# Retention and gated MLP on one core: scores and outputs on 64x64 quarters of TensorE, batch elements in its row halves

## The chip, the core and the metric

The kernel runs on one core of a Trainium2 chip. The core has five engines that run side by side and meet only at semaphores: TensorE (PE, matrix products), VectorE (DVE), ScalarE (ACT), GpSimd (POOL) and SyncE (SP, which here only issues DMAs). Each works through its own instructions in program order. The metric is the device time of one execution in microseconds (us). Before the change it is 214.01 us, the median of 3 runs (213.32 to 214.35).

## The reference

`q`, `k`, `v` have shape (4, 8, 768, 64): batch, heads, sequence, head dimension. Each head keeps a 64x64 state that decays by a factor of its own, and the result goes through an MLP:

```python
gamma = 1.0 - 2.0 ** (-5.0 - np.arange(H))
for t in range(S):
    state = gamma * state + k[:, :, t] (x) v[:, :, t]      # outer product
    y[:, :, t] = scale * q[:, :, t] @ state
...
x = y.transpose(0, 2, 1, 3).reshape(3072, 512)
h = x @ w_in                      # 512 -> 2048
g = h * np.cos(h)
return g @ w_out                  # 2048 -> 512
```

## The kernel before, in words

**Tiling.** The sequence is cut into 6 chunks of 128 positions and the batch into 2 pairs of elements, which makes 12 steps p (0 to 11) of one chunk and one batch pair. `ORDER` maps p to a chunk: p = 0 and 1 are the first chunks of the two pairs, so they have no state before them; all later steps have. Two steps make a group g (0 to 5) of 512 tokens, for which the MLP runs. Everything on PE is bf16, with float32 sums in PSUM. PSUM has 8 banks: one holds the state (`st_ps`), and seven are passed round first in, first out by `Banks`.

**One step p.** `load` brings q, k and v in float32. `conv_q`, `conv_k` and `conv_v` make bf16 copies and fold in the decay. q and k are transposed, by PE for p < 6 (`t_mm`, `t_copy`) and by a DMA issued on SP from p = 6 on (`dma_t`, line 297). `a_mm` (line 331) makes the scores A of a head: 64 rows of contraction, 128 keys by 128 queries. Head 2a stands in rows 0 to 63 and head 2a+1 in rows 64 to 127 of the transposed tiles, so two heads use the two row halves of the array at the same time, with an output bank for each; there are 16 such matmuls in a step. `a_mask` (line 337, DVE) multiplies by the causal mask. `y_mm` (lines 362 and 367) sums two products for each head: state times q, with a state padded by zeros to 128 rows (`stb`), and v times masked scores over 128 keys. Its outputs are 64 partitions high, so two heads stand in the two column halves; a step has 32 of these matmuls, 16 for each of the two products. `y_copy` (ACT) writes `xt`. `s_mm` (line 387) adds the chunk to the state, 16 matmuls of 64 columns, and `s_copy` (line 273 or 271) makes the bf16 state for the next step, in two halves.

**MLP.** `f_mm` (line 401) is one slice of 128 of the 2048 hidden features for 512 tokens, four matmuls of 512 columns; ACT takes the cosine (line 409), DVE multiplies (line 413). `h_mm` (line 422) does two slices for the 256 tokens of a single step, so it needs only that step. `o_mm` (line 446) is a quarter of the contraction of an output tile of 128 tokens; after four of them `o_out` copies the tile (ACT, `ob`) and issues its DMA on SP (line 455).

**The order.** The first part (p = 0 to 5, group 0, parts of p = 6 and 7) is ordered by a planner, `Plan`: each piece of work has a set of engines, a cost, what it comes after, a rank and the banks that it takes; the planner plays this through at build time and emits the pieces by planned start. Where PE would idle early, it puts in matmuls on zeros (`idle_mm`, line 472). In this part the q, k, v and weight loads are issued by POOL, and those of p = 0's k and p = 1's q and k (`"K"`, `"Q1"`, `"K1"`) convert to bf16 on the way. Then, in program order:

```python
plan.emit()
for p in (PL + 2, PL + 3):          # p = 8 and 9
    load(nc.sync, p, "q k v")       # six DMAs on SP
...
for g in range(2, NG + 1):
    for s in range(16):             # f_mm(g, s), then o_mm(g - 1, ...)
        if s % 4 == 3: o_out(g - 1, s // 4, "A")
        if p < NP and r == 3:       # s == 3 and s == 11
            block(p); conv(p + 2); load(nc.sync, p + 4, "q k v")
```

(cut; `conv` has the two `dma_t`, and `conv` and `load` are left out where p + 2 or p + 4 goes past 11.) `block(p)` issues the scores of p + 1, then Y of p with its copies, the state of p, and the masks of p + 1. It runs for p = 6 to 11. So SP's own queue holds, in order: the output DMAs of group 0, the six loads of p = 8 and 9, and then, for each block, an output DMA, two transposes, three loads (for p = 6 and 7) and another output DMA.

Of the kernel before, what the change touches and what calls it, by code (L numbers as in the profile page):

```python
# [146 lines left out]
HALF0, SPARE, RF, RM, COLD = 0, 1, 40.0, 40.0, 8.5  # L147
# [3 lines left out]
def kernel(  # L151
# [39 lines left out]
    st_ps = psum.tile([128, 2, HP, D], FP32, name="st_ps")  # L191
# [13 lines left out]
    qs = [sb([128, 2, H, D], BF16, f"qs{i}") for i in range(NB)]  # L205
    ks = [sb([128, 2, H, D], BF16, f"ks{i}") for i in range(NB)]
    vs = [sb([128, 2, H, D], BF16, f"vs{i}") for i in range(NB)]
    qkt = [sb([128, 2, 2, HP, 128], BF16, f"qkt{i}") for i in range(NB)]
    am = [[[sb([128, HP, 128], BF16, f"am{i}_{b}_{j}") for j in range(2)]
           for b in range(2)] for i in range(2)]  # L210
    stb = [sb([128, 2, HP, 128], BF16, f"stb{i}") for i in range(2)]
# [3 lines left out]
    kx = sb([128, 2, H, D], BF16, "kx")  # L215
# [10 lines left out]
    dec = gtf[:, 2048:4096].bitcast(FP32).rearrange("p (j a t) -> p j a t", j=2, a=HP)  # L226
# [13 lines left out]
    def load(eng, p, names):  # L240

        bp, c = divmod(ORDER[p], NC)
        for n in names.split():
            t, src = SRC[n[0].lower()]
            if len(n) == 1:
                t = (qs[p % NB] if n == "Q" else kb(p)) if n in "QK" else t[p % PRE]
                eng.dma_start(  # L247
                    out=t.rearrange("p b h d -> p (b h) d"),
                    in_=src[ds(2 * bp, 2), :, ds(c * C, C), :].rearrange(
                        "b h t d -> t (b h) d"))  # L250
            else:
                b = int(n[1])
                eng.dma_start(
                    out=t[p % PRE][:, b],
                    in_=src[2 * bp + b, :, ds(c * C, C)].rearrange("h t d -> t h d"))
# [22 lines left out]
    def conv_q(p, b, e):  # L278
        if p < 2:
            copy(e, qs[p % NB][:, b], qf[p % PRE][:, b])  # L280
            return
        ENG[e].tensor_tensor(out=qs[p % NB][:, b], in0=qf[p % PRE][:, b],  # L282
                             in1=bc(gq, ORDER[p] % NC), op=ALU.mult)
# [8 lines left out]
    def conv_k(p, b, e):  # L292
        copy(e, ks[p % NB][:, b], kf[p % PRE][:, b])

    def dma_t(p, w):
        n = p % NB
        nc.sync.dma_start_transpose(
            out=qkt[n][:, w].rearrange("p b a t -> p (b a) t"),
            in_=(qs, ks)[w][n].rearrange("p b h d -> p (b h d)"))
# [3 lines left out]
    def t_mm(p, b, w):  # L303
        if w == 0:
            held["t", p, b] = banks.take()
        tr = held["t", p, b].bitcast(BF16).rearrange("p (w a t) -> p w a t", w=2, a=HP)
        for a in range(HP):
            nc.tensor.transpose(  # L308
                tr[:, w, a, :], (kb(p) if w else qs[p % NB])[:, b, 2 * a : 2 * a + 2, :], ident)

    def t_copy(p, b, w, e):
        bank = held["t", p, b]
        tr = bank.bitcast(BF16).rearrange("p (w a t) -> p w a t", w=2, a=HP)
        copy(e, qkt[p % NB][:, w, b], tr[:, w])
# [3 lines left out]
    def qt(n, b, a):  # L318
        return qkt[n][:, 0, b, a, :]

    def kt(n, b, a):
        return qkt[n][:, 1, b, a, :]

    def a_mm(p, b):
        n = p % NB
        bk = held["a", p, b] = [banks.take(), banks.take()]
        ap = [t.rearrange("p (a t) -> p a t", a=HP) for t in bk]
        for a in range(HP):
            for j in range(2):
                po = 64 * j  # L330
                nc.tensor.matmul(ap[j][:, a, :], lhsT=kt(n, b, a)[po : po + 64, :],  # L331
                                 rhs=qt(n, b, a)[po : po + 64, :],
                                 tile_position=(po, 0))

    def a_mask(p, b, j):
        bank = held["a", p, b][j]
        nc.vector.tensor_tensor(  # L337
            out=am[p % 2][b][j], in0=bank.rearrange("p (a t) -> p a t", a=HP),
            in1=(dec[:, j] if p < 2 else mask.unsqueeze(1).to_broadcast([128, HP, 128])),
# [3 lines left out]
    def a_save(p, b, j):  # L343
        bank = held["a", p, b][j]
# [3 lines left out]
    def a_late(p, b, j):  # L348
        nc.gpsimd.tensor_tensor(out=am[p % 2][b][j],
                                in0=amf[b].rearrange("p (a t) -> p a t", a=HP),  # L350
                                in1=dec[:, j], op=ALU.mult)

    def y_mm(p, b):
        c = ORDER[p] % NC
        n = p % NB
        bank = held["y", p, b] = banks.take()
        v_ = vr[p] if p < 2 else vs[n]
        yp = bank.rearrange("p (a t) -> p a t", a=HP)
        for a in range(HP):
            if c > 0:  # L360
                for j in range(2):
                    nc.tensor.matmul(  # L362
                        yp[ts(j, 64), a, :], lhsT=stb[p % 2][:, b, a, ts(j, 64)],
                        rhs=qt(n, b, a), start=True, stop=False,
                        skip_group_check=True)
            for j in range(2):
                nc.tensor.matmul(  # L367
                    yp[ts(j, 64), a, :], lhsT=v_[:, b, 2 * a + j, :],
                    rhs=am[p % 2][b][j][:, a, :], start=(c == 0), stop=True,
                    skip_group_check=True)  # L370
# [10 lines left out]
    def s_mm(p):  # L381
        x = 1 if p == LATE else p
        for b in range(2):
            for a in range(HP):
                for j in range(2):
                    h = 2 * a + j
                    nc.tensor.matmul(  # L387
                        st_ps[ts(j, 64), b, a, :], lhsT=kb(x)[:, b, h, :],
                        rhs=vb(x)[:, b, h, :],
                        start=(ORDER[x] % NC == 0 and b == 0 and a == 0),  # L390
                        stop=True, skip_group_check=True)

    def s_copy(p, j, e):
        copy(e, stb[(max(p, 1) + 1) % 2][ts(j, 64), :, :, ts(j, 64)], st_ps[ts(j, 64)])
# [54 lines left out]
    def o_out(g, j, e):  # L449
# [5 lines left out]
        nc.sync.dma_start(out=out[ds(o_row(g, j), C), :], in_=o)  # L455
# [14 lines left out]
    def idle_mm(e):  # L470
        bank = banks.take()
        nc.tensor.matmul(bank[:, :256], lhsT=zero[:, :128], rhs=zero, start=True, stop=True)  # L472
# [10 lines left out]
    load(nc.gpsimd, 0, "K")  # L483
    nc.vector.memset(lnsc, math.log(scale))
# [14 lines left out]
    for j in range(2):  # L499
        for a in range(HP):  # L500
            nc.scalar.activation(out=dec[:, j, a, :], in_=dist, func=AF.Exp, bias=lnsc,
                                 scale=float(lg[2 * a + j]))
# [3 lines left out]
    nc.vector.memset(zero, 0.0)  # L506
# [4 lines left out]
    CD = "P"  # L511
    SPLIT = {(1, 0, 1)}
    HOLD = "q2", "o2"
    plan = Plan({"bank": 7, "cos": 3, "sem": 8, "out": 4, "port": 1}, 6.0)
# [7 lines left out]
    ld["q", 0, 0], ld["q", 0, 1], ld["k", 0, 0], ld["k", 0, 1] = map(at, (3.9, 5.0, 6.5, 6.5))  # L522
# [3 lines left out]
    LAG = {"w1": 0.8}  # L526
# [27 lines left out]
    for i in range(2):  # L554
        T["z", i] = add("D", 0.53, lambda e, i=i: nc.vector.memset(stb[i], 0.0), (), 1500, name="z%d" % i)
    for p in range(PL + 2):
        c = ORDER[p] % NC

        for b in range(2):
            if p == 1:  # L560
                T["cq", p, b], T["ck", p, b] = ld["q", p, b], ld["k", p, b]
            else:
                T["cq", p, b] = add("D" if p < 2 else "DP" if p < 3 else "P", SB2 if p < 2 else TT,
# [19 lines left out]
        if p < DMA_T:  # L583
            for b in range(2):
                for w, x in enumerate("qk"):
                    T["t" + x, p, b] = add(
                        "E", 0.225, lambda e, p=p, b=b, w=w: t_mm(p, b, w),
                        [T["c" + x, p, b]] + ([T["tq", p, b]] if w else []), 10 * p + 1,
                        [("bank", 1)] if w == 0 else [], (), "full", name="t%s%d%d" % (x, p, b))
                for w, x in enumerate("qk"):  # L590
                    T["e" + x, p, b] = add(
                        "DA", SB2, lambda e, p=p, b=b, w=w: t_copy(p, b, w, e),
                        [T["t" + x, p, b], T.get(("eq", p, b)) if w else None] + old,
                        10 * p + 0.5, (), [("bank", 1)] if w else [], name="e%s%d%d" % (x, p, b))
            kq = {b: [T["eq", p, b], T["ek", p, b]] for b in range(2)}
        else:
# [4 lines left out]
            kq = {b: [T["dt", p, 0], T["dt", p, 1]] for b in range(2)}  # L601
        if p > PL:
            continue
        ms = []
        if p < ASEP:
            for b in range(2):
                T["a", p, b] = add("E", 0.225, lambda e, p=p, b=b: a_mm(p, b), kq[b], 10 * p + 2,
                                   [("bank", 2)], (), "row", name="a%d%d" % (p, b))
        else:
            T["a", p, 0] = T["a", p, 1] = add(  # L610
                "E", 0.445, lambda e, p=p: (a_mm(p, 0), a_mm(p, 1)), kq[0] + kq[1], 10 * p + 2,
                [("bank", 4)], (), "row", name="a%d" % p)
        for b in range(2):
            for j in range(2):
                if (p, b, j) in SPLIT:
                    o = add("A", (0.49, 0.585), lambda e, p=p, b=b, j=j: a_save(p, b, j),
                            [T["a", p, b]], 0, (), [("bank", 1)],
                            name="ms%d%d%d" % (p, b, j))
                    T["m", p, b, j] = add("P", (1.03, 1.05), lambda e, p=p, b=b, j=j: a_late(p, b, j),
                                          [o], 0, [("port", 1)], [("port", 1)],  # L620
                                          name="ml%d%d%d" % (p, b, j))
                    continue
                T["m", p, b, j] = add("D", (0.6, 0.69), lambda e, p=p, b=b, j=j: a_mask(p, b, j),
                                      [T["a", p, b], G("y", p - 2, b)], 10 * p + 1 + b,
                                      (), [("bank", 1)], name="m%d%d%d" % (p, b, j))
# [157 lines left out]
```

## Time and profile before

| what | value |
|---|---|
| median of the runs | 214.01 us (213.32 to 214.35) |
| the profiled execution's own time | 214.02 us |
| its span, first to last instruction | 212.2 us |
| granted TensorE clock, mean | 1.000 |
| DVE busy | 115.3 us (54%) |
| ACT busy | 115.8 us (55%) |
| POOL busy | 78.6 us (37%) |
| DMA | 32.00 MB, mean 151 GB/s |

"Busy" is the time in which an engine executes something. The span is cut by what runs: 0 to 4.3 us nothing on PE; to 17.6 us the first two steps with fillers; to 73.4 us the rest of the planned part; to 194 us the loop with f and o in turn and a block every 15.7 us; to 208.7 us the last outputs. A view named "chain" follows the work that ended last back to its beginning; a view named "timeline" lists the instructions in order of time, alike ones merged, as start, length, engine, line.

### The profile page before, as it was taken

Reading aid. Unit: us, or ns where it says so; the run is one execution under the profiler, and the core shown is the slowest. Engines: PE = TensorE matmul, PEld = TensorE weight load, DVE = VectorE, ACT = ScalarE, POOL = GpSimd, SP = SyncE. Lnnn points to the kernel's source line nnn. Section 1 sums busy time; section 2 is a strip of 40 time slices with the busy share of each in tenths; the row PEclk is TensorE's granted clock in tenths of the full one; section 3 lists DMA queues with packets and bytes.
Section 4 is the critical chain, followed back from the end, with each engine's and each line's share of the span. In section 5 each row is a group of like instructions: output and inputs, shape, how many; then the busy total and the mean of one; then the engine's idle time right before and its main releaser. Section 6 shows DMA issues by size and latency. Waiting matters only on the chain.

```text
span 212.2 us, 4219 instructions
## 1 busy us (share of the span) xinstructions
PE 202.9 (96%) x1694; PEld 111.4 (52%) x1694; DVE 115.3 (54%) x199; ACT 115.8 (55%) x193; POOL 78.6 (37%) x83
## 2 busy tenths in 40 slices
PE   1899999999999999999999999999999999999993
PEld 1675456798565445445445445446445444444462
DVE  7383898977845635736736636637643333333000
ACT  7485887789663237447547547545535454554120
POOL 8939999979998005533333000000000000000000
PEclk9999999999999999999999999999999999999999
DMA  7999999999998289999993312311011101110212
GB/s 120 197 250 237 297 325 212 221 345 341 345 193 221 78 195 249 256 198 271 159 259 115 88 49 75 78 49 54 7 42 49 53 0 49 49 51 3 99 66 82
DMA packets 57492, 32.00 MB, mean 151 GB/s; under 512 B 46592, under 2 KB 51968, under 8 KB 57472
## 3 DMA queue, kind: packets, MB, share of 16 engines
q0 software_dynamic: 14352, 15.47, 33.0%
q1 hardware_dynamic: 42976, 16.13, 31.2%
q8 instruction: 13, 0.21, 0.4%
q10 hardware_dynamic: 144, 0.13, 0.2%
q14 instruction: 7, 0.06, 0.1%
HBM read 27.26 MB, written 6.29 MB: 158 GB/s over the span
## 4 chain that ended last, share of the span: by engine, by line
PE 91%; DMA 3%; ACT 2%; issue 1%; DVE 1%; POOL 0%; POOLq 0%; DVEq 0%
PE bank L446 38%; PE bank L401 33%; PE bank L422 5%; PE bank L331 3%; DMA ks<-in_k_dram 3%; PE bank L362 3%; PE bank L367 3%; PE bank L308 3%; PE bank L472 2%; PE bank L463 2%; PE st_ps L387 1%; ACT cosb L409 1%; ACT ks L271 1%; ACT xt L271 0%; DVE gt L430 0%
## 5 line engine op out<-in xcount | busy, mean ns | idle before, releaser
L409 ACT ACTIVATE cosb<-bank,halfpi 128x512 bf16<-128x512 f32 x96 | 65.3, 687 | 59.2 <-PE bank L401 55.3
L446 PE MATMUL bank<-w_out_sb,gt 128*128 128x512 bf16 x368 | 90.9, 379 | 0.0
L413 DVE TENSOR_TENSOR gt<-bank,cosb 128x512 bf16<-128x512 f32 x80 | 54.3, 688 | 58.4 <-ACT cosb L409 58.1
L401 PE MATMUL bank<-xt,w_in_sb 128*128 128x512 bf16 x320 | 80.7, 379 | 0.0
L446 PEld LDWEIGHTS <-gt 128*128 128x128 bf16 x368 | 35.7, 98 | 42.4
L401 PEld LDWEIGHTS <-w_in_sb 128*128 128x128 bf16 x320 | 30.5, 98 | 35.1
L286 POOL TENSOR_TENSOR vs<-vf,gk 128x512 bf16<-128x512 f32 x22 | 22.7, 1046 | 12.2 <-DMA vf<-in_v_dram 8.3
L282 POOL TENSOR_TENSOR qs<-qf,gq 128x512 bf16<-128x512 f32 x18 | 18.5, 1045 | 19.5 <-DMA qf<-in_q_dram 19.4
L337 DVE TENSOR_TENSOR am<-bank,mask 128x512 bf16<-128x512 f32 x40 | 24.9, 683 | 1.2 <-PE bank L331 1.0
L271 ACT COPY ob<-bank 128x512 f32<-128x512 f32 (+1 forms) x24 | 13.8, 576 | 17.5 <-PE bank L446 16.1
L273 DVE CAST stb<-st_ps 64x512 bf16<-64x512 f32 x17 | 11.7, 686 | 11.6 <-PE st_ps L387 11.4
L271 ACT CAST xt<-bank 128x512 bf16<-128x512 f32 x24 | 12.9, 589 | 8.4 <-PE bank L367 8.4
L422 PE MATMUL bank<-xt,w_in_sb 128*128 128x256 bf16 x128 | 15.1, 273 | 0.4 <-ACT xt L271 0.4
L422 PEld LDWEIGHTS <-w_in_sb 128*128 128x128 bf16 x128 | 12.2, 98 | 2.0 <-issue 0.6
L271 ACT CAST ks<-kf 128x512 bf16<-128x512 f32 x20 | 11.5, 621 | 0.6 <-DMA kf<-in_k_dram 0.6
L430 DVE TENSOR_TENSOR gt<-bank,cosb 128x512 bf16<-128x512 f32 x16 | 10.4, 684 | 2.2 <-ACT cosb L409 2.2
L362 PE MATMUL bank<-qkt,stb 128*64 128x128 bf16 x160 | 10.3, 222 | 0.0
L367 PE MATMUL bank<-am,vs 128*64 128x128 bf16 x160 | 10.0, 219 | 0.0
L362 PEld LDWEIGHTS <-stb 128*64 128x64 bf16 x160 | 8.7, 110 | 2.4 <-issue 1.9
L247 POOL DMA_DIRECT2D vf<-in_v_dram x8 | 9.4, 1183 | 0.0
L308 PE MATMUL bank<-ident,qs 128*128 128x128 bf16 x48 | 5.2, 250 | 4.4 <-DVE qs L273 4.3
L367 PEld LDWEIGHTS <-vs 128*64 128x64 bf16 x160 | 8.9, 110 | 0.0
(59 smaller groups left out, 116.1 us busy)
## 6 DMA issues: line engine op xcount, KB each, us to landing
out_dram<-ob SPq DMA_DIRECT2D x23, 256.0 KB, 2.0
vf<-in_v_dram POOLq DMA_DIRECT2D x8, 512.0 KB, 8.1
qf<-in_q_dram POOLq DMA_DIRECT2D x6, 512.0 KB, 9.5
kf<-in_k_dram POOLq DMA_DIRECT2D x6, 512.0 KB, 9.3
w_out_sb<-in_moe_w_out_dram POOLq DMA_DIRECT2D x4, 512.0 KB, 10.9
qf<-in_q_dram SPq DMA_DIRECT2D x4, 512.0 KB, 4.6
kf<-in_k_dram SPq DMA_DIRECT2D x4, 512.0 KB, 6.1
vf<-in_v_dram SPq DMA_DIRECT2D x4, 512.0 KB, 6.7
```

Of the source, the lines that this page charges most:

```text
L271: nc.scalar.copy(out=out, in_=in_)
L273: ENG[e].tensor_copy(out=out, in_=in_)
L282: ENG[e].tensor_tensor(out=qs[p % NB][:, b], in0=qf[p % PRE][:, b], in1=bc(gq, ORDER[p] % NC), op=ALU.mult)
L286: ENG[e].tensor_tensor(out=vb(p)[:, b], in0=vf[p % PRE][:, b], in1=bc(gk, ORDER[p] % NC), op=ALU.mult)
L337: nc.vector.tensor_tensor(out=am[p % 2][b][j], in0=bank.rearrange("p (a t) -> p a t", a=HP), in1=(dec[:, j] if p < 2 else mask.unsqueeze(1 ...
L362: nc.tensor.matmul(yp[ts(j, 64), a, :], lhsT=stb[p % 2][:, b, a, ts(j, 64)], rhs=qt(n, b, a), start=True, stop=False, skip_group_check=True)
L367: nc.tensor.matmul(yp[ts(j, 64), a, :], lhsT=v_[:, b, 2 * a + j, :], rhs=am[p % 2][b][j][:, a, :], start=(c == 0), stop=True, skip_group_c ...
L401: nc.tensor.matmul(bank, lhsT=w_in_sb[:, i, ts(f, 128)], rhs=xt[g % 2][:, i, :], start=(i == 0), stop=(i == KIN - 1))
L409: nc.scalar.activation(out=cb, in_=bank, func=AF.Sin, bias=halfpi)
L413: nc.vector.tensor_tensor(out=gt[g % 2][:, f, :], in0=bank, in1=cb, op=ALU.mult)
L422: nc.tensor.matmul(bank[:, ts(e, 256)], lhsT=w_in_sb[:, i, ts(f + e, 128)], rhs=xt[g % 2][:, i, ts(hf, 256)], start=(i == 0 and e == 0), s ...
L446: nc.tensor.matmul(bank, lhsT=gt[g % 2][:, f, ts(j, 128)], rhs=w_out_sb[:, f, :], start=(f == 0), stop=(f == KOUT - 1))
```

## The change

The two batch elements now stand in the two row halves: the transposed tiles hold, for each head, element 0 in partitions 0 to 63 and element 1 in 64 to 127. A is cut into 64x64 quarters (32 matmuls for a step, row half = batch element, column half = half of the keys). Y with a state uses quarters too: state times q with 64 rows and no padding, and v times scores in two halves of the keys; for the second half of the keys only the last 64 queries are computed. [...] The zeros of `stb` go, and its copy is one instruction. The three converting loads become two DMAs each. The output DMA is taken out of `o_out` and issued at the end of the loop's body, behind block, transposes and loads. Seven matmuls on zeros of 512 columns are put ahead of everything on PE, and the planner's constants change: `HALF0` from 0 to 4 (the first four slices of group 0 are done as h for p = 0 and p = 1 apart), one more mask of p = 0 goes by ACT and POOL, and assumed times of the first loads and engines.

```diff
-HALF0, SPARE, RF, RM, COLD = 0, 1, 40.0, 40.0, 8.5
+HALF0, SPARE, RF, RM, COLD = 4, 1, 40.0, 40.0, 5.2
...
-    qs = [sb([128, 2, H, D], BF16, f"qs{i}") for i in range(NB)]
-    ks = [sb([128, 2, H, D], BF16, f"ks{i}") for i in range(NB)]
+    qs = [sb([128, H, 2, D], BF16, f"qs{i}") for i in range(NB)]
+    ks = [sb([128, H, 2, D], BF16, f"ks{i}") for i in range(NB)]
...
-    stb = [sb([128, 2, HP, 128], BF16, f"stb{i}") for i in range(2)]
+    stb = [sb([128, H, D], BF16, f"stb{i}") for i in range(2)]
...
-                t = (qs[p % NB] if n == "Q" else kb(p)) if n in "QK" else t[p % PRE]
+                if n in "QK":
+                    for b in range(2):
+                        eng.dma_start(
+                            out=(qs[p % NB] if n == "Q" else kb(p))[:, :, b, :],
+                            in_=src[2 * bp + b, :, ds(c * C, C)].rearrange("h t d -> t h d"))
+                    continue
...
         for a in range(HP):
-            for j in range(2):
-                po = 64 * j
-                nc.tensor.matmul(ap[j][:, a, :], lhsT=kt(n, b, a)[po : po + 64, :],
-                                 rhs=qt(n, b, a)[po : po + 64, :],
-                                 tile_position=(po, 0))
+            h = 4 * u + a
+            for x in range(2):
+                for b in range(2):
+                    nc.tensor.matmul(ap[b][ts(x, 64), a, :], lhsT=kt(n, b, h)[:, ts(x, 64)],
+                                     rhs=qt(n, b, h), tile_position=(64 * b, 64 * x),
+                                     skip_group_check=True)
...
+    def intra(p, b, a, x, **kw):
+
+        ms = []
+        for j in range(2):
+            h = 2 * a + j
+            ms.append(nc.tensor.matmul(
+                held["yp", p][b][ts(j, 64), a, 64 * x :], lhsT=vs[p % NB][ts(x, 64), b, h, :],
+                rhs=am[p % 2][b][h // 4][ts(x, 64), h % 4, 64 * x :],
+                start=False, stop=True, tile_position=(64 * x, 64 * j), skip_group_check=True))
+        return ms
+
+    def y1_mm(p):
+        bk = [banks.take(), banks.take()]
+        held["y", p, 0], held["y", p, 1] = bk
+        held["yp", p] = [t.rearrange("p (a t) -> p a t", a=HP) for t in bk]
+        for a in range(HP):
+            for b in range(2):
                 for j in range(2):
+                    h = 2 * a + j
                     nc.tensor.matmul(
+                        held["yp", p][b][ts(j, 64), a, :], lhsT=stb[p % 2][ts(b, 64), h, :],
+                        rhs=qt(p % NB, b, h), start=(a == 0), stop=False,
+                        tile_position=(64 * b, 64 * j), skip_group_check=True)
+        for a in range(HP):
+            held["part", p] = intra(p, 1, a, 1) + intra(p, 0, a, 0)
+
+    def hop(p):
+        ms = held["part", p]
+        held["hop", p] = nc.sync.nop(nofuse=True)
+        for m in ms:
+            after(m, held["hop", p])
+
+    def y2_mm(p):
+        for a in range(HP):
+            for m in intra(p, 1, a, 0) + intra(p, 0, a, 1):
+                if a == 0:
+                    after(held["hop", p], m)
...
-    def s_copy(p, j, e):
-        copy(e, stb[(max(p, 1) + 1) % 2][ts(j, 64), :, :, ts(j, 64)], st_ps[ts(j, 64)])
...
+    def s_copy(p, e):
+        copy(e, stb[(max(p, 1) + 1) % 2], st_ps)
...
-        nc.sync.dma_start(out=out[ds(o_row(g, j), C), :], in_=o)
+        held["dma", g, j] = o
+
+    def o_dma(g, j):
+        nc.sync.dma_start(out=out[ds(o_row(g, j), C), :], in_=held.pop(("dma", g, j)))
...
+    for i in range(7):
+        idle_mm("E", 2)
...
+    MERGE = 5
+    CQ, CD = "D", "P"
+    SPLIT = {(1, 0, 1), (0, 1, 1)}
...
     def block(p):
         nxt = p + 1 < NP
+        y1_mm(p)
+        hop(p)
         if nxt:
             a_mm(p + 1, 0)
             a_mm(p + 1, 1)
+        y2_mm(p)
         for b in range(2):
-            y_mm(p, b)
             y_copy(p, b, "A")
         if has_s(p):
             s_mm(p)
...
                     conv(p + 2)
                 if p + 4 < NP:
                     load(nc.sync, p + 4, "q k v")
+            if s % 4 == 3:
+                o_dma(g - 1, s // 4)
```

`after(x, m)` makes m wait for x. The loads of p = 8 and 9 stay where they were, between the planned part and the loop.

## The prediction

> **What bounds the kernel now.** I read four views in this order: the page's busy times and chain, its costliest groups, the timeline of PE around one block, and the timeline of SP.
>
> ```profile
> PE 202.9 (96%) x1694; PEld 111.4 (52%) x1694; DVE 115.3 (54%) x199; ACT 115.8 (55%) x193; POOL 78.6 (37%) x83
> PE 91%; DMA 3%; ACT 2%; issue 1%; DVE 1%; POOL 0%; POOLq 0%; DVEq 0%
> L446 PE MATMUL bank<-w_out_sb,gt 128*128 128x512 bf16 x368 | 90.9, 379 | 0.0
> ```
>
> PE is the bound: 96% busy, 91% of the chain, and its costliest group has no idle time before it. By the view of waits it stands still only at the start (4.3 us for the first q, 0.6 for k) and for 0.4 us near 36 us. So what PE no longer does is gained, and what it newly waits for is lost, at full price, from 17.6 us on.
>
> The timeline of PE around block p = 6 (start, length, line, count):
>
> ```profile
> 79.49 1.03 PE L446 MATMUL bank<-w_out_sb,gt 128*128 128x512 bf16 x4
> 80.44 0.62 PE L331 MATMUL bank<-qkt 64*128 64x128 bf16 x16
> 81.00 0.25 PE L362 MATMUL bank<-qkt,stb 128*64 128x128 bf16 x2
> 81.08 0.22 PE L367 MATMUL bank<-am,vs 128*64 128x128 bf16 x2
> 81.13 0.22 PE L362 MATMUL bank<-qkt,stb 128*64 128x128 bf16 x2
> ...
> 81.91 0.42 PE L387 MATMUL st_ps<-vx,kx 128*64 128x64 bf16 x16
> 82.26 1.04 PE L401 MATMUL bank<-xt,w_in_sb 128*128 128x512 bf16 x4
> ```
>
> Lengths include the run through the array, so rates come from starts. Y issues a pair of column halves every 0.055 us (81.08, 81.13). A: 0.62 less the 0.225 of one (its group's mean), over 15 steps, is 26.6 ns each, again a pair in about 0.055. State: 0.42 less 0.196, over 15, is 14.9 ns each. In the chain the block is A 0.55, Y 1.02, state 0.25 and 0.11 extra in the next f: 1.93 us. A is 8 pairs of 0.055 (0.445) and Y 16 (0.89), so about 0.1 goes at each change of array shape.
>
> The timeline of SP shows where the new no-op has to queue:
>
> ```profile
> 71.66 2.92 SPq L455 DMA_DIRECT2D out_dram<-ob  x2
> 74.68 0.39 SPq L247 DMA_DIRECT2D qf<-in_q_dram  x1
> 75.16 1.63 SPq L247 DMA_DIRECT2D kf<-in_k_dram  x1
> 76.89 2.63 SPq L247 DMA_DIRECT2D vf<-in_v_dram  x1
> 79.60 2.32 SPq L247 DMA_DIRECT2D qf<-in_q_dram  x1
> 82.02 1.77 SPq L247 DMA_DIRECT2D kf<-in_k_dram  x1
> 83.88 2.39 SPq L247 DMA_DIRECT2D vf<-in_v_dram  x1
> 86.36 1.96 SPq L455 DMA_DIRECT2D out_dram<-ob  x1
> ```
>
> and of ACT, the copy that the last of these DMAs sends:
>
> ```profile
> 80.55 0.58 ACT L271 COPY ob<-bank 128x512 f32<-128x512 f32 x1 [0.17 <-DMA kf<-in_k_dram]
> ```
>
> That tile was ready at 81.13 and its DMA began at 86.36, as soon as the sixth load was through. A load takes 0.39 us when nothing is queued and 1.6 to 2.6 behind others, and each starts 0.1 us after the one before it ends. SP works in order and its loads hold it.
>
> **The change, part by part**
>
> *Quarters.* A goes from 16 matmuls in 8 pairs to 32 in 8 fours; Y from 32 in 16 pairs to 16 + 16 + 16 in 12 fours. The trace has no fours. Bounds: no faster than pairs (27.7 ns each), 80 x 27.7 = 2.2 us against 1.33 now, +0.9 for a step; or a four every 0.055 us, 20 x 0.0555 = 1.11, -0.22. The state's matmuls, 14.9 ns each, show that issue is not the limit at 27 ns; a four wants 13.9. At 14.9 the step would gain 0.14. I take -0.22, nearest to the state's row.
>
> Loads of weights of 64 columns go at the state's rate too, 16 in the same 0.25 us. [...]
>
> *Shape changes, about 0.1 each.* Block before: to rows, to columns, back. After: to quarters, to columns for the state, back. Equal. For p = 5 scores of p = 6 join Y: one fewer. For p = 2, 3 and 4 the state stands between the two parts of Y: two more, which eats the 0.22. So blocks 6 to 10: -5 x 0.22 = -1.1; p = 5: -0.3; p = 2 to 4: 0.
>
> *The wait inside Y, SP free.* From a matmul's modelled end to its reader the trace has 0.04 us (the state's matmuls of p = 7 end at 98.07, their DVE copy starts at 98.11) and its end is 0.22 after its issue; engine to PE is 0.05 (the xt copy ends 35.86, h starts 35.91). SP's own no-op is in no row: between 0 and 0.33, an idle SP's shortest DMA issue. So 0.31 to 0.64 against a cover of 0.055 + 0.445 (scores between): 0 to 0.14 for each of blocks 5 to 10. I take 0 with a no-op of 0.1; if not, at most 0.8 in all. Block 11 has no scores between: about +0.3, less its 0.22: +0.1.
>
> *The wait inside Y, SP not free.* Queued on SP ahead of the no-op of p = 6 are the two output DMAs and all six loads. PE's loop starts at 73.44; eight pieces of 0.8645 bring the block at 80.4, then 0.1 + 0.445 (first part) + 0.445 (scores): PE is at the second part at 81.4. The sixth load ends at 86.27, the no-op passes at about 86.4. **Stall: 5.0 us.** Everything behind waits: y copies, state, f of s = 4. Loop and loads both hang on the last output tile of group 0 (the loads start 1.24 after the loop), so an earlier loop moves both. The three loads of p = 10 took 4.6 us for half the bytes when less was in flight; at that rate six take 9.2, and the stall is 2.6. So 2.6 to 5.0; I take 5.0, since these six are the same six.
>
> Block 7 then reaches its second part at 86.4 + 15.5 = 101.9. Ahead of its no-op on SP: two transposes after the k copy (ACT behind the y copies, about 89), 2.8; three loads, 4.6; two output DMAs, 3.9: free at about 100.4. Block 8, by the same sum, has 1 us to spare; later blocks have no loads. So 0, with 0 to 1.5 as range. In the planned part SP has transposes of 1.3 us and waits for their copies near p = 4 and 5: 0 to 1.3, I take 0.2.
>
> *Clock after the stall.* Granted clock is 1.000 in every slice, yet scores took 1.03 us at 9.11 and 0.62 at 12.76: after the idle first 4.3 us PE ran at half rate until about 11. A 5 us stall may bring that back: 0 to 3.3 us (half of 6.6). That stretch was only partly filled, dense work follows here; I take 0.8. [...]
>
> *Start.* Issuing 512 KB costs POOL 1.17, a w_in quarter 0.82; half a load I put at 0.95, so three split loads delay what POOL issues next by 3 x (1.9 - 1.17) = 2.2 us. Landings are 1.5 apart (7.46, 9.1, 10.8, then v at 12.4 and 13.9) while issues are 1.15 apart, so transfers set the pace and about 1.0 remains: v of p = 1 at 15, w_in 15.14 -> 16.2. Against that PE is warm when k lands: transposes 1.03 and scores 0.96 take half, about -1.0, so Y of p = 1 stays near 16. Two h pieces (1.74 us) take the place of fillers until 17.6: PE is 1.2 ahead. But at 35.46 PE runs out of f and waits for Y of p = 2, a chain that starts with q landing at 24.6. Most of the 1.2 waits there. I take -0.5; bounds -1.9 (all h and no delay) and +1.5 (p = 2's loads late as well).
>
> *At nothing.* One state copy instead of two (0.69 saved on DVE) and no zeros: DVE is 54% busy. Strided bf16 outputs: the strided state copy on ACT (0.58) is no slower than plain ones (0.58 to 0.62). Output DMAs later: `ob` has four buffers, each used again 31 us later.
>
> **Sum**, on the profiled execution (214.02, span 212.2; the median is 214.01): -1.1 - 0.3 + 0.1 + 5.0 + 0.2 + 0.8 - 0.5 = +4.2: **218.2 us**.
>
> **The rivals**
>
> *Faster: the loads do not hold the no-op.* One mechanism, at the no-op of p = 6: if SP hands its loads on quickly (0.4 each, as the first did), it is free at 77.2, before PE needs it at 81.4. Then 214.02 - 1.1 - 0.3 + 0.1 + 0.2 - 0.5 = 212.4. It decides when the stall is under 1.6 us, six loads in 8.2 us or less instead of 11.6. For: a single load takes 0.4. Against: the 5.2 us that the ready tile waited. With a start at its better bound this gives 211.
>
> *The quarters do not run four at a time.* Ten steps at +0.9 and the scores of p = 0 and 1 at +0.45: +9.9, with stall, clock and start 214.02 + 9.9 + 5.0 + 0.8 - 0.5 = 229.2. For: no fours in the trace. Against: the state's 14.9 ns.
>
> *The stall is there, but shorter and better paid.* Loads at the faster rate (2.6), no cold clock, start at -1.5: 214.02 - 1.3 + 2.6 + 0.2 - 1.5 = 214.0, no change.
>
> **Numbers.** Stall at about full length 0.58; stall short, about the same time 0.12; no stall, faster 0.23; quarters in pairs 0.07. Within the forecast 216.5 to 220.5 by its bounds. The range 211.8 to 220.5 takes in all but pairs and the ends of the others. Under 0.5% a measurement of this kernel can't be told from no change: faster 0.24, same 0.11, slower 0.65.
>
> **What would show it.** Right: PE idle for some 5 us within the block of p = 6, released by SP, in a slice near 82 us; SP's timeline with the no-op behind the load of v; scores of 32 in 0.55 to 0.6 us; Y's parts at 14 ns a matmul; the later blocks without idle and 15.5 us apart; f-sized work from about 16.3 us. Wrong: no idle there (loads issue faster or SP passes them), pairs of 28 ns in the quarters, or h of p = 2 starting much before or after 35.9 us.

## The result, and the profile after

The changed kernel takes 220.72 us (median of 4 runs, 220.34 to 221.30) against 214.18 for the kernel before (4 runs): a ratio of 1.030, 95% interval 1.023 to 1.037. That is slower, as forecast, but by 6.5 us instead of 4.2, and 0.2 above the stated range. The profiled execution took 220.34 us, its span 218.6.

The page of the changed kernel, in the order busy times, granted clock in 40 slices, chain by engine, and the group of v times scores:

```profile
PE 206.2 (94%) x2080; PEld 112.9 (52%) x2080; DVE 110.6 (51%) x188; ACT 115.6 (53%) x192; POOL 81.8 (37%) x87
PEclk9999999999999996799999999999999999999999
PE 81%; SPq 5%; DMA 4%; POOL 3%; DVE 3%; ACT 1%; issue 1%; POOLq 0%; DVEq 0%; ACTq 0%
L386 PE MATMUL bank<-am,vs 64*64 64x128 bf16 (+1 forms) x320 | 8.3, 209 | 5.3 <-SPq L409 5.2
```

Two things are new: the chain now has 5% on SP's queue, which had none, and one group of matmuls has 5.3 us of idle time ahead of it, 5.2 of them released by the no-op of line 409. The granted clock (PEclk, in tenths of full speed), full throughout before, dips in two slices near 85 and 90 us.

That no-op is `hop`. In a step with a state, v times scores runs in two parts that swap banks, `y1_mm` and `y2_mm`, with `hop` between them on SP: it waits for the last matmuls of the first part, and the first matmuls of the second part wait for it. In `block` (up to p = 10) and for p = 5 the scores of p + 1 are put between the parts, for p = 2 to 4 the state's matmuls.

The timeline of PE in block p = 6 of the changed kernel (start, length, line, count; in brackets the idle time before it and what ended that; L400 state times q, L386 v times scores, L338 scores of p = 7, L432 state):

```profile
80.47 0.42 PE L400 MATMUL bank<-qkt,stb 64*64 64x128 bf16 x16
80.71 0.33 PE L386 MATMUL bank<-am,vs 64*64 64x128 bf16 x14
80.84 0.22 PE L338 MATMUL bank<-qkt 64*64 64x128 bf16 x2
80.88 0.22 PE L386 MATMUL bank<-am,vs 64*64 64x128 bf16 x2
80.90 0.69 PE L338 MATMUL bank<-qkt 64*64 64x128 bf16 x30
86.81 0.63 PE L386 MATMUL bank<-am,vs 64*64 64x128 bf16 x16 [5.22 <-SPq L409]
87.37 0.64 PE L432 MATMUL st_ps<-vx,kx 128*64 128x64 bf16 x16
87.94 1.89 PE L444 MATMUL bank<-xt,w_in_sb 128*128 128x512 bf16 x4
89.62 1.49 PE L489 MATMUL bank<-w_out_sb,gt 128*128 128x512 bf16 x4
90.95 1.03 PE L444 MATMUL bank<-xt,w_in_sb 128*128 128x512 bf16 x4
```

and SP's timeline beside it (L252 the six loads, L304 a transpose; the no-op is not listed):

```profile
74.70 0.39 SPq L252 DMA_DIRECT2D qf<-in_q_dram  x1
75.19 2.82 SPq L252 DMA_DIRECT2D kf<-in_k_dram  x1
78.10 1.77 SPq L252 DMA_DIRECT2D vf<-in_v_dram  x1
79.97 2.57 SPq L252 DMA_DIRECT2D qf<-in_q_dram  x1
82.62 1.71 SPq L252 DMA_DIRECT2D kf<-in_k_dram  x1
84.42 2.28 SPq L252 DMA_DIRECT2D vf<-in_v_dram  x1
89.64 1.25 SPq L304 DMA_TRANSPOSE qkt<-ks  x1
```

The chain in order of time shows the no-op between the sixth load and PE:

```profile
84.42 2.28 SPq L252
86.70 0.05 issue
86.75 0.02 SPq L409
86.76 0.04 issue
86.81 0.63 PE bank L386 x7
```

The sixth load ends at 86.70 and the second part of Y starts at 86.81. Then the state takes 0.64 instead of 0.42, and the next f and o 1.89 and 1.49 instead of 1.03: PE runs at half rate, with a granted clock of 0.50, until about 90.5. Stretches of the changed kernel (length, busy time and count of PE, PEld, DVE, ACT, POOL, then the granted clock):

```profile
83.00:83.50 0.50, 0.00 (x0) 0.00 (x0) 0.00 (x0) 0.00 (x0) 0.00 (x0) 1.00 0.63 144
83.50:84.00 0.50, 0.00 (x0) 0.00 (x0) 0.00 (x0) 0.00 (x0) 0.00 (x0) 0.72 0.85 195
88.00:90.00 2.00, 2.00 (x7) 0.67 (x6) 1.95 (x4) 1.74 (x5) 0.60 (x1) 0.50 1.03 234
90.40:90.60 0.20, 0.20 (x2) 0.12 (x1) 0.20 (x2) 0.16 (x1) 0.00 (x0) 0.64 0.55 82
```

Away from the two changes the clock reads 1.00 or 0.50 here, so the mean of 0.72 puts the fall at 83.72, that is 2.1 us after the last matmul ended (86.81 - 5.22 = 81.59), and the mean of 0.64 puts the return at 90.54.

**Where the 6.4 us between the two spans lie** (218.6 against 212.2). Each number is a difference of starts in the two timelines.

| stretch | before | after | difference |
|---|---|---|---|
| h of p = 2 starts | 35.91 | 36.49 | +0.58 |
| from there to the loop's first f | 37.53 | 36.98 | -0.55 |
| from there to block 6 | 7.00 | 7.00 | 0 |
| block 6 to block 7 | 15.74 | 22.66 | +6.92 |
| block 7 to block 11, 4 blocks | 62.95 | 62.25 | -0.70 |
| block 11 to the end of the span | 53.1 | 53.2 | +0.1 |

Block 6 alone holds more than all of it. Block 7 of the same kernel, which has no stall, is the measure for it:

```profile
103.13 0.42 PE L400 MATMUL bank<-qkt,stb 64*64 64x128 bf16 x16
104.05 0.42 PE L386 MATMUL bank<-am,vs 64*64 64x128 bf16 x16
118.69 0.42 PE L400 MATMUL bank<-qkt,stb 64*64 64x128 bf16 x16
```

There the second part of Y starts 0.92 after the block, and the next block 14.64 after that. In block 6 the two are 6.34 (80.47 to 86.81) and 16.32 (86.81 to 103.13). So the stall costs 5.42 and the half clock 1.68; a block gains 0.18 elsewhere (15.56 against 15.74), and 5.42 + 1.68 - 0.18 = 6.92. The 5.22 of the view is less than 5.42 because it counts from the modelled end of the last matmul.

### The profile page after: what moved, and what is told of

It reads as the page before. It is cut to its first block, busy times and chain, and to the rows that moved or that the text cites. A ratio compares the mean times of both kernels' runs of the same rounds, so it can differ in the third digit from the quotient of the medians.

```text
span 218.6 us, 4964 instructions
## 1 busy us (share of the span) xinstructions
PE 206.2 (94%) x2080; PEld 112.9 (52%) x2080; DVE 110.6 (51%) x188; ACT 115.6 (53%) x192; POOL 81.8 (37%) x87
## 4 chain that ended last, share of the span: by engine, by line
PE 81%; SPq 5%; DMA 4%; POOL 3%; DVE 3%; ACT 1%; issue 1%; POOLq 0%; DVEq 0%; ACTq 0%
PE bank L489 35%; PE bank L444 27%; PE bank L465 8%; SPq L252 5%; DMA vf<-in_v_dram 4%; PE bank L386 2%; PE bank L338 2%; PE bank L314 2%; PE st_ps L432 2%; PE bank L509 2%; PE bank L400 1%; DVE am L344 1%; POOL ks L248 1%; POOL qs L248 1%; POOL kx L248 1%
## 5 line engine op out<-in xcount | busy, mean ns | idle before, releaser
L444 PE MATMUL bank<-xt,w_in_sb 128*128 128x512 bf16 x304 | 77.7, 383 | 0.0
L444 PEld LDWEIGHTS <-w_in_sb 128*128 128x128 bf16 x304 | 29.1, 98 | 34.4 <-issue 0.6
L465 PE MATMUL bank<-xt,w_in_sb 128*128 128x256 bf16 x160 | 18.6, 273 | 1.1 <-ACT xt L276 1.1
L465 PEld LDWEIGHTS <-w_in_sb 128*128 128x128 bf16 x160 | 15.4, 98 | 3.6 <-issue 1.4
L278 DVE CAST stb<-st_ps 128x512 bf16<-128x512 f32 x10 | 6.9, 688 | 18.4 <-PE st_ps L432 18.4
L386 PE MATMUL bank<-am,vs 64*64 64x128 bf16 (+1 forms) x320 | 8.3, 209 | 5.3 <-SPq L409 5.2
L518 PE MATMUL bank<-zero 128*128 128x256 bf16 (+1 forms) x64 | 11.6, 324 | 1.3 <-DVE halfpi L534 1.1
L252 POOL DMA_DIRECT2D vf<-in_v_dram x8 | 9.4, 1188 | 0.0
L518 PEld LDWEIGHTS <-zero 128*128 128x128 bf16 x64 | 6.5, 108 | 4.6 <-issue 2.7
L386 PEld LDWEIGHTS <-vs 64*64 64x64 bf16 x320 | 5.8, 110 | 5.8 <-SPq L409 5.6
L338 PE MATMUL bank<-qkt 64*64 64x128 bf16 x384 | 8.3, 218 | 0.0
```

Of the source, the lines that this page charges most:

```text
L252: eng.dma_start(out=t[p % PRE].rearrange("p b h d -> p (b h) d"), in_=src[ds(2 * bp, 2), :, ds(c * C, C), :].rearrange("b h t d -> t (b h) ...
L386: ms.append(nc.tensor.matmul(held["yp", p][b][ts(j, 64), a, 64 * x :], lhsT=vs[p % NB][ts(x, 64), b, h, :], rhs=am[p % 2][b][h // 4][ts(x, ...
L444: nc.tensor.matmul(bank, lhsT=w_in_sb[:, i, ts(f, 128)], rhs=xt[g % 2][:, i, :], start=(i == 0), stop=(i == KIN - 1))
L465: nc.tensor.matmul(bank[:, ts(e, 256)], lhsT=w_in_sb[:, i, ts(f + e, 128)], rhs=xt[g % 2][:, i, ts(hf, 256)], start=(i == 0 and e == 0), s ...
L518: nc.tensor.matmul(bank[:, : 256 * n].rearrange("p (n t) -> p n t", n=n), lhsT=zero[:, :128], rhs=zero.unsqueeze(1).to_broadcast([128, n, ...
```

## The experiments

Theory 1: the no-op of p = 6 waits on SP behind the six loads, PE waits for the no-op, and the idle PE loses its clock. The rivals put the time elsewhere. Times are medians; the kernel before, run beside them, had 214.1 to 214.3.

**The no-op on another engine.**

```diff
-        held["hop", p] = nc.sync.nop(nofuse=True)
+        held["hop", p] = (nc.sync if p < 6 else nc.gpsimd).nop(nofuse=True)
```

> The changed kernel with one edit: the no-op inside Y stands on GpSimd instead of SP for p = 6 to 11, where GpSimd's queue is empty at that time. Theory 1 (the no-op of p = 6 waits on SP behind six loads, and the idle PE then loses its clock): the stall of 5.2 us and the 1.75 us at half clock go, no PE idle in block 6, loop blocks 15.56 us apart, 220.7 - 7.0 = about 213.7 us. Rival (the split of Y and the quarters themselves cost the time, on whatever engine the no-op stands): still 219 to 221 us.

Measured: 213.14 us (10 runs), ratio to the kernel before 0.996 (0.993 to 0.999). PE's timeline in block 6 of this kernel:

```profile
80.80 0.69 PE L338 MATMUL bank<-qkt 64*64 64x128 bf16 x30
81.28 0.42 PE L386 MATMUL bank<-am,vs 64*64 64x128 bf16 x16
81.64 0.44 PE L432 MATMUL st_ps<-vx,kx 128*64 128x64 bf16 x16
```

The second part of Y follows the scores with no idle time, and the state is back at 0.44. One engine name is worth 7.6 us, and the rest of the change, taken together, is a gain of 0.4%, hardly more than nothing. The rival has fallen: split and quarters, with the rest, cost no time.

**PE kept busy in the gap.**

```diff
+        if p == 6:
+            for i in range(24):
+                idle_mm("E", 2)
         y2_mm(p)
```

> The changed kernel plus 24 matmuls of 512 columns on zeros (5.2 us) on PE between the scores and the second part of Y of p = 6; the no-op stays on SP. Adds work that the reference does not need. If the slow stretch after the stall (granted clock 0.50) comes from PE standing idle: the stall's length stays, the clock stays 1.00, 220.7 - 1.75 = about 219.0 us. If it comes from something else that the stall brings (late copies, transfers): f of s = 4 still takes 1.9 us and the time stays at 220.7.

Measured: 218.48 us (4 runs). Two stretches of this kernel inside the gap, in the columns from above:

```profile
82.00:84.00 2.00, 2.00 (x12) 0.87 (x9) 0.00 (x0) 0.00 (x0) 0.00 (x0) 1.00 0.95 216
84.00:86.00 2.00, 2.00 (x11) 0.87 (x9) 0.00 (x0) 0.00 (x0) 1.94 (x2) 1.00 1.07 243
```

The clock stays at 1.00, the second part of Y still starts only at 86.38, and o behind it takes 1.03 again. 24 useless matmuls make the kernel 2.2 us faster: the half clock came from standing idle and was a price of its own. Not all of the difference is that price. Of the 2.11 us between the two profiled executions 0.56 is a block 6 that starts earlier here (79.91 against 80.47), ahead of the edit, and the stall is 0.13 longer; 1.68 is left, the same as above.

**One load fewer ahead** (v of p = 9 issued behind block 6):

```diff
-    for p in (PL + 2, PL + 3):
-        load(nc.sync, p, "q k v")
+    load(nc.sync, 8, "q k v")
+    load(nc.sync, 9, "q k")
...
                 block(p)
+                if p == 6:
+                    load(nc.sync, 9, "v")
```

> The changed kernel with the last of the six loads (v of p = 9) issued behind block 6 instead of ahead of the loop. Theory 1: the no-op passes when the fifth load is through, near 84.4, so the stall is 5.2 - 2.4 = about 2.8 us; if the clock only falls after some 3 us of idleness it stays at 1.00: 220.7 - 2.4 - 1.75 = 216.6. If the clock falls all the same: 218.3. Rival (stall not set by the loads): 220.7.

Measured: 216.85 us (4 runs), two of them at 215.7 and 215.9 and two at 217.8 and 218.2. PE's timeline:

```profile
83.98 0.41 PE L386 MATMUL bank<-am,vs 64*64 64x128 bf16 x16 [2.37 <-SPq L409]
```

The fifth load ends at 83.88 and the stall is 2.37: it follows the queue's length. The profiled run is one of the two shorter ones, in which the granted clock was 1.000; in the two longer ones it was 0.989 and 0.990. Both answers that were put down came out: with this queue the clock fell in two of four executions. How long PE stood idle in the two longer ones is not known, and a limit of some 3 us of idleness, which was supposed beforehand, is shown by no run.

**The wait without the change.** The kernel before, with one no-op in its block 6 (`m` is a matmul of state times q):

```diff
...
-                nc.tensor.matmul(ap[j][:, a, :], lhsT=kt(n, b, a)[po : po + 64, :],
+                held["last"] = nc.tensor.matmul(ap[j][:, a, :], lhsT=kt(n, b, a)[po : po + 64, :],
...
+                    if p == 6 and b == 0 and a == 0:
+                        after(held["hop"], m)
...
             a_mm(p + 1, 0)
+            if p == 6:
+                held["hop"] = nc.sync.nop(nofuse=True)
+                after(held["last"], held["hop"])
             a_mm(p + 1, 1)
```

> The kernel before, with nothing of the change but one no-op on SP in block 6: it waits for the first half of the scores of p = 7, and the first matmuls of Y of p = 6 wait for it. Theory 1: the no-op stands behind the same six loads, PE idles from about 81.0 to 86.4, 5.3 us, then 1.75 us at half clock: 214.2 + 7 = about 221 us. Rival (the wait hurts only because of the quarters, the swapped banks or the later output DMAs): within 0.5 us of 214.2.

Measured: 222.62 us (4 runs, 221.18 to 225.44); without the longest of them the ratio is 1.038 (1.030 to 1.045). PE's and SP's timelines:

```profile
89.58 0.32 PE L367 MATMUL bank<-qkt,stb 128*64 128x128 bf16 x2 [6.77 <-SPq L718]
```

```profile
84.94 2.15 SPq L247 DMA_DIRECT2D vf<-in_v_dram  x1
87.19 2.29 SPq L462 DMA_DIRECT2D out_dram<-ob  x1
```

Row and column halves, no quarters, and the loss is there. The wait is longer than the 5.3 us expected, since in this kernel an output DMA stands ahead of the no-op too: the sixth load ends at 87.09, the output DMA at 89.48. That is the DMA which the change moved behind the block. (This execution reached block 6 at 82.19 instead of 80.44, loads and all, for a reason that no run shows.)

**That DMA put back ahead of the block**, in the changed kernel:

```diff
                 o_out(g - 1, s // 4, "A")
+                o_dma(g - 1, s // 4)
...
-            if s % 4 == 3:
-                o_dma(g - 1, s // 4)
```

> The changed kernel with the output DMA of the loop issued right behind its copy again, so ahead of the block and its no-op, as in the kernel before. It tells what moving it was worth. Theory 1: the no-op of p = 6 has one more DMA of about 2.0 us ahead, stall 7.2 instead of 5.2: 222.7 us; later blocks as before. Rival (the output DMA is handed on at once): 220.7.

Measured: 224.03 us (4 runs), 3.3 more than the changed kernel. The second part in blocks 6 and 7:

```profile
88.52 0.63 PE L386 MATMUL bank<-am,vs 64*64 64x128 bf16 x16 [6.86 <-SPq L409]
105.68 0.41 PE L386 MATMUL bank<-am,vs 64*64 64x128 bf16 x16
```

Expected were 2.0. Only 1.6 of the difference is the longer stall of block 6 (6.86 against 5.22). In blocks 7 to 10 of this kernel the second part also starts about 0.25 us late (in block 7 at 105.68, where 105.42 would be right behind the scores), and block 11 waits 0.52; the sum had left both out. So moving the output DMA is also what makes the no-op free in the later blocks.

**All loads of p = 9 behind block 6**, the no-op left on SP:

```diff
-    for p in (PL + 2, PL + 3):
-        load(nc.sync, p, "q k v")
+    load(nc.sync, 8, "q k v")
...
                 block(p)
+                if p == 6:
+                    load(nc.sync, 9, "q k v")
```

> The changed kernel with all three loads of p = 9 issued behind block 6; the no-op stays on SP. Theory 1 by the same sum over SP's queue: three loads end near 80, before PE's second part at 81.6, so no stall in block 6 and no half clock; behind it SP has three loads, two transposes, three loads and two output DMAs until about 97, when block 7 needs its no-op: 0 to 0.6 us there; 220.7 - 7.0 + 0 to 0.6 = 213.7 to 214.3. Rival (SP itself is a bad place for the no-op, whatever is ahead): over 216.

Measured: 215.07 us (10 runs), seven from 214.3 to 215.6 and three from 217.0 to 217.3, between the two numbers that were put down. In the profiled run, one of the three, block 6 has no stall, but block 7 has one. Its PE timeline and two stretches:

```profile
99.00 0.41 PE L386 MATMUL bank<-am,vs 64*64 64x128 bf16 x16 [1.84 <-SPq L409]
```

```profile
100.00:100.50 0.50, 0.50 (x3) 0.20 (x2) 0.50 (x2) 0.50 (x3) 0.00 (x0) 0.57 1.06 405
103.00:104.00 1.00, 1.00 (x5) 0.35 (x3) 0.53 (x1) 0.00 (x0) 0.00 (x0) 0.76 0.98 220
```

The sum over SP's queue was right in kind (the stall moves to the next block) and 1.2 us short in size; a transpose took 4.23 us behind the loads, the next one 1.25. And 1.84 us of idleness was followed by half clock from about 100.07 to 103.48, after PE had already begun again. In the three longer runs the granted clock was 0.992, in the seven others 1.000. Here moving loads within one queue (215.07) was a worse cure than another queue (213.14).

**The start.** The table has h of p = 2 later by 0.58. The chain that it waits for is late by as much; the masks of p = 2 on DVE and this h, in the kernel before and then in the changed one:

```profile
30.21 2.47 DVE L337 TENSOR_TENSOR am<-bank,mask 128x512 bf16<-128x512 f32 x4
35.91 1.03 PE L422 MATMUL bank<-xt,w_in_sb 128*128 128x256 bf16 x8 [0.45 <-ACT xt L271]
```

```profile
30.79 2.48 DVE L344 TENSOR_TENSOR am<-bank,mask 128x512 bf16<-128x512 f32 x4
36.49 1.91 PE L465 MATMUL bank<-xt,w_in_sb 128*128 128x256 bf16 x16 [1.12 <-ACT xt L276]
```

Four kernels look into it, all with the no-op of p >= 6 on GpSimd. First without the early halves:

```diff
-HALF0, SPARE, RF, RM, COLD = 4, 1, 40.0, 40.0, 5.2
+HALF0, SPARE, RF, RM, COLD = 0, 1, 40.0, 40.0, 5.2
```

> The kernel of e1 (no-op on GpSimd) with HALF0 back at 0: no slice of group 0 is done as h for p = 0 ahead of p = 1. Theory (the start is bound by the chain of p = 2, from q landing near 24.6 to its y copy at 36.4, and what PE gains ahead of it is waited away there): PE's 1.1 us wait near 36 us gets shorter by about what is lost before, the loop still starts within 0.3 of 73.4, 213.1 us. Rival (the early halves are worth what they fill): loop about 1.2 us later, 214.3.

Measured: 213.07 us (10 runs), ratio 0.995 (0.991 to 0.998): as fast as with them (213.14). The lines are of the kernel with halves (no-op on GpSimd), then of the one without, where h of p = 2 starts:

```profile
36.39 1.91 PE L465 MATMUL bank<-xt,w_in_sb 128*128 128x256 bf16 x16 [1.11 <-ACT xt L276]
```

```profile
35.80 1.03 PE L465 MATMUL bank<-xt,w_in_sb 128*128 128x256 bf16 x8
```

Work done earlier is waited for 18 us later. The early halves bring nothing. In the profiled execution the loop even starts at 72.86 without them, against 73.37 with them, more than the 0.3 either way that was expected; the medians show no such difference.

Then q of p = 2 loaded earlier:

```diff
-    HOLD = "q2", "o2"
+    HOLD = "w2", "o2"
...
-    LOADS = ["Q1", "K1", "v0", "v1", "w0a", "w0b", "w1", "w2", "q2", "k2", "w3a", "v2", "w3b", "q3", "k3", "v3",
+    LOADS = ["Q1", "K1", "v0", "v1", "w0a", "w0b", "w1", "q2", "w2", "k2", "w3a", "v2", "w3b", "q3", "k3", "v3",
```

> The kernel of e1 with the load of q of p = 2 issued ahead of the w2 weights, and w2 held behind the late mask in its place. Theory (start bound by the chain of p = 2): q lands 2 us or more earlier, PE's 1.1 us wait near 36 us goes, the loop starts about 1.1 us earlier, 212.0 us. Rival (bound by weights or by PE's own work): w2 comes late, PE waits for it instead, 213.1 or more.

Measured: 213.56 us (10 runs), no gain. q was issued at 12.6 instead of 15.2 and converted from 22.2 on instead of 24.65, yet Y of p = 2 started at 33.16 (32.96 with the no-op on GpSimd alone). PE transposed q of p = 2 at 24.59 instead of 27.27, but k, which the scores need too, at 28.49 instead of 28.17. So q's landing is not what the chain waits for here. k of p = 2 was converted at 26.69 in this kernel and 26.33 in the other, hardly moved, which fits k, but no run moved k. Y of p = 1 became late as well: a conversion of v on DVE took 2.29 us, where it took 1.17 in the changed kernel.

Then both edits together:

> The kernel of e6 with HALF0 back at 0. With e1, e5 and e6 it makes a square: if the chain of p = 2 was what ate the early halves, they are worth about 1 us here (this run 1 us slower than e6) and nothing without the early q. If they are worth nothing here too, something else eats them.

Measured: 214.58 us (10 runs), 1.0 above the run before. That is the number that was put down for theory, but the square does not decide: theory also wanted the early q to gain 1.1 us, and it gained nothing. And in both kernels with the early q PE waits for DVE in Y of p = 1 (1.26 us with the early halves, 1.13 without), which the other two kernels do not have, so the halves may be worth something here for that reason.

And without the early zeros:

```diff
-    for i in range(7):
-        idle_mm("E", 2)
```

> The kernel of e1 without the seven matmuls on zeros of 512 columns at the start (the planner's own fillers stay). PE's first transposes and scores then run at half the clock. Theory (start bound by the chain of p = 2): loop start within 0.3 of 73.4, 213.1 us. Rival (the early warm clock is worth the half of those rows, about 1 us): 214.1.

Measured: 213.66 us (10 runs), ratio 0.997 (0.994 to 0.999); the loop's first f starts at 73.39 against 73.37 with the zeros. Of the work that was expected to run slow, PE's first transposes took 1.04 us (at 5.17), the next ones 0.61 (at 8.51) and the first scores, at 9.60, 0.64 as with the zeros: only those first transposes were slow. The early matmuls on zeros do nothing that lasts until the loop. The median lies between the two numbers that were put down, but against the kernel before it can't be told from that of the kernel with the zeros (0.996, 0.993 to 0.999).

## Why the prediction was right and wrong

- **The stall: right.** 5.0 was said, 5.42 measured from start to start, by the mechanism named (e1, e3, e4). The sum's end of the sixth load (86.27, against 86.70) is the 0.4.
- **The clock: a step that failed, in size.** "That stretch was only partly filled, dense work follows here; I take 0.8." The 0.8 was the author's estimate, and no run shows it: the loss was 1.68, in the profile and again against the profile with zeros in the gap (e2). Dense work did not shorten it: the half clock held until 90.5, 3.7 us into that work. The bounds of the term (0 to 3.3) held the value, but the stated range did not take them in: 218.2 with the clock at 3.3 is 220.7. All four runs of the changed kernel had the low clock (mean granted clock 0.981 to 0.984); in e9, as far as one trace shows, 1.84 us of idleness were enough.
- **The start: the other step that failed, and the larger in size.** -0.5 was said; h of p = 2 started 0.58 later, 1.1 off. The prediction took the chain of p = 2 to stay where it was and PE's lead to be partly kept. In the changed kernel that chain is late by the same 0.58 (masks of p = 2 at 30.79 instead of 30.21), and PE waits 1.12 us for it instead of 0.45. Early halves and early zeros show no gain (e5, e8), as the argument about the wait near 36 us had it, but the value then taken, a gain of 0.5, went against that argument. That the chain waits for q is refuted by e6. Without the early halves h starts at 35.80, so the delay may come with them; what makes the chain late stays open.
- **Quarters: right in kind.** Y's first part and the scores are 64 matmuls from 103.13 to 104.05, 14.4 ns each, against 13.9 assumed. A block gains 0.18 us, not 0.22: -0.88 instead of -1.1 over five blocks.
- **Planned part: better than said.** From h of p = 2 to the loop 0.55 less, where 0.3 for p = 5, 0 for p = 2 to 4 and +0.2 for waits were put down. No wait on SP shows there. It makes up for 0.45 of the 1.1 at the start: together the two put the loop's first f 0.03 later than before, where 0.6 earlier was said.
- **Free no-op: right.** The scores hide it in blocks 7 to 10 (second part at 104.05, right behind the scores). Block 11, with nothing between, loses 0.1, as said.

By these sizes: -0.88 - 0.55 + 0.58 + 0.1 + 5.42 + 1.68 = 6.35, against 6.4 between the two spans. The forecast of +4.2 missed by 0.4 in the stall, 0.9 in the clock, 1.1 at the start and 0.2 in the quarters, less 0.45 in the planned part.

The rivals: "the loads do not hold the no-op" fell to the stall itself, to e3 and to e4; "the quarters do not run four at a time" fell to the 14.4 ns; "shorter and better paid" fell to the full stall with its half clock.

## What to carry to other kernels

The wait that went by way of a third engine cost what was queued on that engine: six loads held SP's queue from 74.70 to 86.70, 12 us that appear in none of the page's busy times; PE stood still for 5.22 us behind it, and the same no-op on an engine whose queue was empty at that moment made the kernel 7.6 us faster. So put such a relay on an engine whose queue is empty when it is needed, and count every instruction ahead of it. When PE would stand idle, price the clock with it (1.68 us on top of a wait of 5.22; 1.84 us of idleness lost the clock in one profiled execution, 2.37 us did not in another), or give PE something to do, as the 24 matmuls on zeros did (2.2 us faster). Work pulled forward only counts if whatever comes after it is not waiting for something else: the early halves were waited away, with 213.14 us against 213.07 without them.

## What the runs showed that was not expected

The low clock lasted nearly the same time in three traces and half of it in a fourth. In the changed kernel it ran from 83.72 to 90.54, in the kernel before with the no-op from 85.54 to 92.37, in the kernel with the output DMA ahead from 84.74 to 91.56, and in the one with three loads ahead from 100.07 to 103.48: 6.82, 6.83, 6.82 and 3.41 us. These times come from the means of stretches that a change falls into, as above; the second and the third kernel's:

```profile
85.40:85.60 0.20, 0.00 (x0) 0.00 (x0) 0.00 (x0) 0.00 (x0) 0.20 (x1) 0.86 1.27 288
92.00:92.40 0.40, 0.40 (x1) 0.14 (x1) 0.40 (x1) 0.40 (x2) 0.40 (x1) 0.54 0.00 0
```

```profile
84.50:85.00 0.50, 0.00 (x0) 0.00 (x0) 0.00 (x0) 0.00 (x0) 0.50 (x1) 0.74 1.20 271
91.50:92.00 0.50, 0.50 (x4) 0.20 (x2) 0.50 (x2) 0.42 (x1) 0.50 (x2) 0.94 0.00 0
```

The fall does not keep one distance from the idleness: it came 2.1, 2.7 and 3.1 us after PE's last matmul in the first three, and in the last after PE had been idle for 1.84 us and working again for 1.07. What sets the moment of the fall and the length of the low clock, no run shows. Nor does the length of the idleness alone decide: 1.84 us lost the clock in one profiled execution, 2.37 us kept it in another. By the granted clock of every run it fell in 4 of 4 runs of the changed kernel, in 2 of 4 with five loads ahead and in 3 of 10 with three.

And the clock row is full in the first slices of the kernel before, where its matmuls take nearly twice their later time (the 16 scores of a step 1.03 us at 9.11, 0.62 at 12.76): the row did not show that stretch, and why is open.
